# Second-layer weight sums in a lane of their own, GpSimd in program order for two token groups, and closing additions moved into the last products

## The chip, the cores and the metric

One Trainium2 chip, one of its cores. The time is the device time of one execution in microseconds (us), the median of three runs.

The engines by the names of the profile: PE (TensorE matmul, with PEld for its weight loads), DVE (VectorE), ACT (ScalarE), POOL (GpSimd), SP (SyncE, which here issues every DMA).

## The reference, cut to what matters

Three stages follow each other: an attention between tokens and a small state, a two-layer block (`_moe_ref`), and a mixture of eight experts. The change lies in the last one:

```python
def _moe2_ref(x, w_gate, w1, w2):          # x: 2304 x 512 in the signature; 2176 tokens here
    logits = x @ w_gate
    P = np.exp(logits - logits.max())
    for _ in range(8):                      # rows, then columns, eight times
        P /= P.sum(1, keepdims=True) + 1e-09
        P /= P.sum(0, keepdims=True) + 1e-09
        P *= N / E
    for e in range(8):
        h = np.maximum(x @ w1[e], 0.0)      # 512 -> 1024
        out += P[:, e:e + 1] * (h @ w2[e])  # 1024 -> 512
```

All products are made at nearly full float32 precision: a factor is written as a rounded part (hi) and the rest (lo), and three matmuls (hi times lo, hi times hi, lo times hi) stand for one.

## The kernel before, in words

**Units.** The tokens are cut into three groups, g = 0, 1, 2, of 768, 768 and 640 tokens; an expert's 1024 hidden columns are cut into four pieces of 256. One pair of a group and a piece is a unit, s = 0 to 95, with s // 32 the group and s % 32 the piece. `experts()` walks over the units. In this execution unit 0 begins near 444 us, unit 32 near 1030 us, unit 64 near 1498 us.

**PE in a unit.** The first layer of a unit (`quad`) is made with seven block products instead of eight: m1, m6, m5, m7, m2, m4, m3, in this order, six matmuls each, in three banks px, py and pz. m6 leaves its product in py; DVE adds it to m1's (tile u), and only then may m7 accumulate into the same bank py, so m7 waits for that u. In group 0 the second layer is plain: after the first products of a unit stand the six token tiles of the unit before (`layer2_moe`, bank po, six matmuls of 512 columns each). In groups 1 and 2 the second layer has seven products too (`product`, bank pm, order P1, P2, P3, P7, P5, P6, P4), which DVE adds up over the 32 units in the tiles m; after the last unit of a group seven additions between those tiles (`combine`), a transposition (`rows`, bank pt) and the stores give the output.

**Weights in group 0.** `weights_a(s + 1)` and `weights_b(s)` run beside the matmuls of unit s. `weights_a` takes the raw first weights (rw), makes four sums of quarters on POOL (tile sum), and splits weights and sums: hi by ACT (wah, wsh), lo by POOL (wal, wsl). `weights_b` splits the raw second weights (w2h by ACT, w2l by POOL, two pieces of 128x512), makes four sums on DVE (tile sumb, lines L694 to L698) and splits them in two pairs wz_0 and wz_1: hi by ACT (L768), lo by DVE (L769). Everything is also stored to DRAM (`keep`), since groups 1 and 2 load it again (`again`) in place of making it.

**The order.** Between matmul groups `slot()` advances each lane (a list of generators) by one step; a generator's `yield n` says how many slots it rests. A unit of group 0 has 13 slots, one of groups 1 and 2 has 14. `weights_a` and `weights_b` of a unit stand behind each other in lane "w". PE, ACT and, in `experts()`, DVE run in the order in which the code is written; for POOL and SP a scheduler chooses the order when the program is built.

**Memory.** A tile is taken by its tag; tiles of one tag share one place (or `bufs` places in turn), and a new one waits for all readers of the old one, the store by `keep` among them. wz_0 and wz_1 share tag "z" with one place until unit 5; in units 6 to 29 wz_1 lies in "xl5". `sumb` shares "y" with the tile sum until unit 5.

**Late in group 0.** From unit 26 on `sums_of(1)` makes eight differences of 128x384 on DVE for group 1, and in unit 31 `forms(1)` splits the seven token forms of group 1: hi by ACT (L630), lo by DVE (L634, 128x768 each). After group 1 `finish(1)` runs its seven additions on POOL (L976, 128x768) while group 2 computes; after group 2 `finish_last` runs them on DVE and then transposes and stores six row tiles.

Of the kernel before, what the change touches and what calls it, by code (L numbers as in the profile page):

```python
# [19 lines left out]
P = 128  # L20
# [7 lines left out]
FU = 256  # L28
# [16 lines left out]
def body(ctx: ExitStack, tc: tile.TileContext, xt_in, xn_in, stb, stk, wd, ws, alpha, wgate, out):  # L45
# [645 lines left out]
    def sums_left(eng, out, a11, a12, a22, a21):  # L691

        s1, s2, s3, s4 = (out[:, i, :] for i in range(4))
        eng.tensor_tensor(out=s1, in0=a21, in1=a22, op=ALU.add)  # L694
        eng.tensor_tensor(out=s2, in0=s1, in1=a11, op=ALU.subtract)  # L695
        yield 1
        eng.tensor_tensor(out=s3, in0=a11, in1=a21, op=ALU.subtract)  # L697
        eng.tensor_tensor(out=s4, in0=a12, in1=s2, op=ALU.subtract)  # L698
# [31 lines left out]
    def weights_b(s):  # L730
# [23 lines left out]
        if s < 6:  # L754
# [197 lines left out]
    def product(s, i):  # L952
# [26 lines left out]
    def rows(g, h, t0, nt):  # L979

        blocks = [("P2", "P4"), ("P3", "P7")][h]
        ps = p2["tr"].tile([P, 512], F32, tag="tr", name=f"pt{g}_{h}_{t0}")
# [26 lines left out]
    def finish(g):  # L1009

        yield 14
        yield from combine(g, nc.gpsimd, 12)
        yield 12
# [103 lines left out]
    later, soon, lanes = [], [], {"x": [], "state": [], "gate": [], "early": [], "sums": [], "blocks": [], "v": [], "w": [], "h": [], "out": []}  # L1117
# [181 lines left out]
    def experts():  # L1299

        nonlocal pb
        after = ["B11", "T2", "T1", "T3", "B21", "T4", "B22"]
        for s in range(NS2 + 1):
# [20 lines left out]
            if s < NS2:  # L1324
                lanes["w"].append(weights_b(s))
# [102 lines left out]
```

## Time and profile before

| | |
|---|---|
| three runs | 1934.12, 1934.17, 1934.86 us; median 1934.17 us |
| the profiled execution | 1936.51 us, its span 1934.7 us |
| busy, share of the span | PE 94%, PEld 87%, DVE 77%, POOL 64%, ACT 38% |
| granted TensorE clock, mean | 0.971 |

The profile is of one execution. Its span runs from the first to the last instruction; 1.8 us lie around it. Busy shares are means over stages that are limited in different ways, so the rows below are cut by stage, and a stage is read by what PE waits for in it.

### The profile page before, as it was taken

How to read it: one execution, taken by the hardware profiler on the slowest of the kernel's cores; microseconds unless marked ns; L12 is line 12 of the kernel's file. 1: busy time of each engine (PE TensorE's matmuls, PEld its weight loads, DVE VectorE, ACT ScalarE, POOL GpSimd, SP SyncE). 2: the span in 40 equal slices, each digit the busy share in tenths (PEclk: the TensorE clock that was granted, in tenths of full speed). 3: DMA queues.
4: the chain of work that ended last, by engine and by line, in shares of the span. 5: the costliest groups of instructions: out<-in, count | busy, mean ns of one | idle time of the engine just before them, and what ended most of it. 6: DMA issues, size and time to landing. Idle time of an engine off the chain costs nothing.

```text
span 1934.7 us, 29731 instructions
## 1 busy us (share of the span) xinstructions
PE 1813.7 (94%) x10179; PEld 1678.3 (87%) x10179; DVE 1482.3 (77%) x2323; ACT 736.4 (38%) x1397; POOL 1235.8 (64%) x1300
## 2 busy tenths in 40 slices
PE   6799999988889999999999999999999899999997
PEld 5688888876768888888778999999999899999996
DVE  6645777775788888888877777887788777778886
ACT  6755666643223333333332222222223233333332
POOL 4423555565447666666654777777777877777774
PEclk8799999998989999999999999999999899999998
DMA  5111111114557877787778777777777589888882
GB/s 213 44 50 50 50 55 48 41 71 159 206 207 264 289 283 278 281 287 280 256 281 296 248 264 267 247 261 273 250 259 255 199 304 316 315 313 302 304 298 98
DMA packets 179813, 423.82 MB, mean 219 GB/s; under 512 B 20288, under 2 KB 37184, under 8 KB 179664
## 3 DMA queue, kind: packets, MB, share of 16 engines
q1 hardware_dynamic: 179664, 421.94, 61.7%
q8 instruction: 81, 1.33, 0.3%
q14 instruction: 68, 0.56, 0.1%
HBM read 299.92 MB, written 121.94 MB: 218 GB/s over the span
## 4 chain that ended last, share of the span: by engine, by line
PE 48%; POOL 12%; issue 7%; DVE 5%; DMA 3%; ACT 1%; SPq 0%; POOLq 0%; ACTq 0%; DVEq 0%
PE pm L964 22%; PE py L801 10%; PE px L801 7%; PE pz L801 7%; POOL wsl L671 3%; POOL w2l L671 3%; PE po L1071 3%; POOL wal L671 2%; DMA kept_bl<-wz 2%; POOL sum L694 1%; POOL sum L695 1%; POOL sum L697 1%; DVE g2l L824 1%; DMA rw<-in_ws_dram 1%; PE pt L984 0%
## 5 line engine op out<-in xcount | busy, mean ns | idle before, releaser
L970 DVE TENSOR_TENSOR m<-pm,m 128x768 f32<-128x768 f32 (+1 forms) x434 | 384.0, 885 | 136.4 <-PE pm L964 136.0
L964 PE MATMUL pm<-formgh,wz 128*128 128x384 f32 (+1 forms) x1152 | 216.5, 323 | 0.7 <-POOL formgh L905 0.5
L801 PE MATMUL py<-rT,wsh 128*128 128x384 f32 (+1 forms) x768 | 193.8, 335 | 24.8 <-DVE u L808 24.8
L895 POOL TENSOR_TENSOR formgh<-mid,formgh 128x384 fp32r<-128x384 f32 (+1 forms) x128 | 121.7, 952 | 123.4 <-ACT formgh L894 102.4
L964 PEld LDWEIGHTS pm<-formgh,wz 128*128 128x128 f32 x1152 | 190.1, 188 | 1.3 <-POOL formgh L905 0.7
L801 PE MATMUL px<-rB,wah 128*128 128x384 f32 (+1 forms) x768 | 190.3, 330 | 0.2 <-DVE c L808 0.2
L823 ACT ACTIVATE g2h<-c 128x384 fp32r<-128x384 f32 x96 | 50.4, 525 | 335.2 <-DVE c L808 335.2
L801 PEld LDWEIGHTS py<-rT,wsh 128*128 128x128 f32 x768 | 136.2, 191 | 37.0 <-DVE u L808 36.1
L536 POOL TENSOR_TENSOR gl<-r,gh 128x512 fp32r<-128x512 f32 (+1 forms) x80 | 94.2, 1191 | 115.0 <-ACT gh L535 61.8
L671 POOL TENSOR_TENSOR wal<-rw,wah 128x256 fp32r<-128x256 f32 x96 | 77.1, 830 | 128.9 <-ACT wah L669 94.0
L1071 PE MATMUL po<-w2h,g2l 128*128 128x512 f32 x384 | 153.2, 399 | 2.0 <-DVE g2l L824 1.8
L1071 PE MATMUL po<-w2l,g2h 128*128 128x512 f32 x384 | 154.9, 403 | 0.0
L1071 PE MATMUL po<-w2h,g2h 128*128 128x512 f32 x384 | 154.2, 402 | 0.0
L801 PEld LDWEIGHTS px<-rB,wah 128*128 128x128 f32 x768 | 138.1, 191 | 6.8 <-DVE c L808 0.5
L905 POOL TENSOR_TENSOR T<-mid,mid 128x384 f32<-128x384 f32 (+1 forms) x128 | 119.8, 958 | 30.4 <-DVE mid L889 30.4
L894 ACT ACTIVATE formgh<-mid 128x384 fp32r<-128x384 f32 (+1 forms) x128 | 63.9, 499 | 181.6 <-DVE mid L889 131.6
L551 PE MATMUL po<-gl,wh 128*128 128x512 f32 (+1 forms) x320 | 120.4, 377 | 13.1 <-DVE acc L568 11.1
L1093 DVE SCALAR_TENSOR_TENSOR oa<-po,pr,oa 128x512 f32<-128x512 f32 x168 | 122.8, 742 | 10.2 <-PE po L1071 9.6
L801 PE MATMUL py<-rT,wsl 128*128 128x384 f32 (+1 forms) x384 | 126.9, 330 | 0.0
L801 PE MATMUL px<-rB,wal 128*128 128x384 f32 (+1 forms) x384 | 126.2, 329 | 0.0
L964 PE MATMUL pm<-formgl,w2h 128*128 128x384 f32 (+1 forms) x512 | 123.3, 324 | 2.3 <-DVE m L970 2.3
L905 POOL TENSOR_TENSOR T<-mid,T 128x384 f32<-128x384 f32 (+1 forms) x128 | 121.7, 951 | 5.1
(240 smaller groups left out, 5126.5 us busy)
## 6 DMA issues: line engine op xcount, KB each, us to landing
wsh<-kept_ah SPq DMA_DIRECT2D x64, 512.0 KB, 4.5
wsl<-kept_al SPq DMA_DIRECT2D x64, 512.0 KB, 5.4
wz<-kept_bh SPq DMA_DIRECT2D x128, 256.0 KB, 5.0
wz<-kept_bl SPq DMA_DIRECT2D x128, 256.0 KB, 5.1
wah<-kept_ah SPq DMA_DIRECT2D x64, 384.0 KB, 3.2
wal<-kept_al SPq DMA_DIRECT2D x64, 384.0 KB, 3.8
w2h<-kept_bh SPq DMA_DIRECT2D x64, 384.0 KB, 6.0
w2l<-kept_bl SPq DMA_DIRECT2D x64, 384.0 KB, 6.6
```

Of the source, the lines that this page charges most:

```text
L536: nc.gpsimd.tensor_tensor(out=lo, in0=r, in1=f32(hi), op=ALU.subtract)
L551: nc.tensor.matmul(ps, lhsT=w2(wt, u, f, d * P, P), rhs=g[:, f, :n], start=(i == 0), stop=(i == 3 * NF - 1))
L671: nc.gpsimd.tensor_tensor(out=lo[:, i], in0=src[:, i], in1=f32(hi[:, i]), op=ALU.subtract)
L801: nc.tensor.matmul(bank[b], lhsT=w[:, k * P:(k + 1) * P], rhs=xf[:, j, k, :], start=(first and i == 0), stop=(i == 5), skip_group_check=True,)
L823: nc.scalar.activation(out=hi, in_=src, func=AF.Relu)
L894: nc.scalar.activation(out=hi, in_=out, func=AF.Copy)
L895: nc.gpsimd.tensor_tensor(out=lo, in0=out, in1=f32(hi), op=ALU.subtract)
L905: nc.gpsimd.tensor_tensor(out=out, in0=x, in1=y, op=ALU.subtract)
L964: nc.tensor.matmul(ps[:, q, :n], lhsT=w[:, q * P:(q + 1) * P], rhs=x, start=(j == 0), stop=(j == 2))
L970: nc.vector.tensor_tensor(out=mm[g][name], in0=ps[:, :, :n], in1=mm[g][name], op=ALU.add)
L1071: nc.tensor.matmul(ps, lhsT=x[:, f, t * P:(t + 1) * P], rhs=w[:, f, :], start=(i == 0), stop=(i == 3 * NF - 1))
L1093: nc.vector.scalar_tensor_tensor(out=a, in0=ps, scalar=p, in1=a, op0=ALU.mult, op1=ALU.add)
```

## The change

1. `weights_b` gets a lane of its own, "w2", from unit 2 on, so that it begins at the first slot of a unit, beside `weights_a`. Its four sums are spread over four slots, and the hi of a pair (ACT) and its lo (DVE) stand one slot apart.
2. wz_1 lies in "xl3" (units 2 to 25) or "xl5" (26 to 30), apart from wz_0; `sumb` lies in "xh5" from unit 2 on. For that the broadcast row tile pb is taken at unit 31 in place of 30, and its loads are issued one unit ahead in place of two.
3. The lo parts of the forms T2, T3 and T4 of group 1 move from DVE to POOL.
4. From unit 32 on POOL runs in the order of the code.
5. `finish(1)` rests 20 slots and then 14 between additions (before: 14 and 12).
6. The seven closing additions of group 2 are moved: two to POOL and three to DVE within the last unit's products, two to DVE between the two halves of the rows. The rows of the last group take turns in the two places of bank m, and the second tile of each half is copied out by DVE.

```diff
@@ forms(g): put
-                nc.vector.tensor_tensor(out=t[:, 1, part], in0=src[:, part], in1=f32(t[:, 0, part]), op=ALU.subtract)
+                eng = nc.gpsimd if g == 1 and name in ("T2", "T3", "T4") else nc.vector
+                eng.tensor_tensor(out=t[:, 1, part], in0=src[:, part], in1=f32(t[:, 0, part]), op=ALU.subtract)
@@ weights_b
-        if s < 6:
+        if s < 2:
             sums = p2["t"].tile([P, 4, FU], F32, tag="y", name=f"sumb{s}", bufs=1)
...
-        yield from sums_left(nc.vector, sums, halves[:, 0, 0], halves[:, 1, 0], halves[:, 1, 1], halves[:, 0, 1])
+        yield from sums_left(nc.vector, sums, halves[:, 0, 0], halves[:, 1, 0], halves[:, 1, 1], halves[:, 0, 1], 1)
...
-            if i and 6 <= s < U2 - 2:
-                z = big.tile([P, 2, 2, FU], F32R, tag="xl5", name=f"wz_{s}_{i}")
+            if i and s >= 2 and s != U2 - 1:
+                z = big.tile([P, 2, 2, FU], F32R, tag="xl3" if s < U2 - 6 else "xl5", name=f"wz_{s}_{i}")
...
             nc.scalar.activation(out=hi, in_=src, func=AF.Copy)
+            yield 1
             nc.vector.tensor_tensor(out=lo, in0=src, in1=f32(hi), op=ALU.subtract)
             keep(u, "b", (hi, lo), 3 + 2 * i)
-            yield 2
+            yield 1
@@ product
+        if s == NS2 - 1:
+            for eng, after, x, y in (
+                (nc.gpsimd, "P2", "P2", "P1"), (nc.gpsimd, "P5", "P3", "P5"), (nc.vector, "P6", "P6", "P1"),
+                (nc.vector, "P6", "P7", "P6"), (nc.vector, "P6", "P4", "P7"),
+            ):
+                if after == name:
+                    join(eng, g, x, y)
@@ finish
-        yield 14
-        yield from combine(g, nc.gpsimd, 12)
-        yield 12
+        yield 20
+        yield from combine(g, nc.gpsimd, 14)
@@ finish_last
-        for _ in combine(g, nc.vector, 0):
-            pass
...
+            if h:
+                join(nc.vector, g, "P7", "P5")
+                join(nc.vector, g, "P3", "P6")
...
+                if k == 1:
+                    nc.vector.tensor_copy(out=t[:nt], in_=ps[:nt])
+                else:
+                    nc.scalar.activation(out=t[:nt], in_=ps[:nt], func=AF.Copy)
@@ experts
+            if s == U2:
+                pool_order = tc.manual_schedule(engines={mybir.EngineType.Pool})
+                pool_order.__enter__()
...
-                lanes["w"].append(weights_b(s))
+                lanes["w2" if s > 1 else "w"].append(weights_b(s))
```

What it does to the order is shown at three places. In the rows g2l is the lo of the hidden layer, c and u are sums of products, oa the output rows, and the number behind a name is the unit.

DVE in the second half of unit 12, up to the u that m6 of unit 13 needs, before:

```order
L698 TENSOR_TENSOR sumb_6347<-rw_12_6198,sumb_6347 128x256
L808 TENSOR_TENSOR c_12_6367<-py_6255,p_12_6246 128x384
L769 TENSOR_TENSOR wz_0_6372<-sumb_6347,wz_0_6372 128x512
L1093 SCALAR_TENSOR_TENSOR oa_4301<-po_11_4_6377,pr,oa_4301 128x512
L824 SCALAR_TENSOR_TENSOR g2l_6238<-c_12_6367,g2h_6237 128x384
L808 TENSOR_TENSOR c_12_6392<-pz_6282,u_12_6262 128x384
L769 TENSOR_TENSOR wz_1_6395<-sumb_6347,wz_1_6395 128x512
L1093 SCALAR_TENSOR_TENSOR oa_4301<-po_11_5_6400,pr,oa_4301 128x512
L824 SCALAR_TENSOR_TENSOR g2l_6238<-c_12_6392,g2h_6237 128x384
L808 TENSOR_TENSOR u_13_6434<-py_6427,p_13_6418 128x384
```

and after:

```order
L775 TENSOR_TENSOR wz_0_6347<-sumb_6293,wz_0_6347 128x512
L1116 SCALAR_TENSOR_TENSOR oa_4301<-po_11_3_6359,pr,oa_4301 128x512
L830 SCALAR_TENSOR_TENSOR g2l_6238<-px_6239,g2h_6237 128x384
L814 TENSOR_TENSOR c_12_6376<-py_6266,p_12_6246 128x384
L775 TENSOR_TENSOR wz_1_6368<-sumb_6293,wz_1_6368 128x512
L1116 SCALAR_TENSOR_TENSOR oa_4301<-po_11_4_6382,pr,oa_4301 128x512
L830 SCALAR_TENSOR_TENSOR g2l_6238<-c_12_6376,g2h_6237 128x384
L814 TENSOR_TENSOR c_12_6397<-pz_6295,u_12_6273 128x384
L1116 SCALAR_TENSOR_TENSOR oa_4301<-po_11_5_6400,pr,oa_4301 128x512
L830 SCALAR_TENSOR_TENSOR g2l_6238<-c_12_6397,g2h_6237 128x384
L814 TENSOR_TENSOR u_13_6445<-py_6438,p_13_6418 128x384
```

Both lo steps moved up by three to four instructions, and their hi is now issued on ACT one slot earlier; the sums, which stood in the middle of the unit, now begin behind its first oa.

POOL around the start of unit 12 (sum and wal, wsl of unit 13's first weights, w2l of the second weights), before:

```order
L694 TENSOR_TENSOR sum_6252<-rw_13_6133 128x256
L697 TENSOR_TENSOR sum_6252<-rw_13_6133 128x256
L695 TENSOR_TENSOR sum_6252<-sum_6252,rw_13_6133 128x256
L698 TENSOR_TENSOR sum_6252<-rw_13_6133,sum_6252 128x256
L671 TENSOR_TENSOR w2l_6149<-rw_11_6026,w2h_6148 128x512 x2
L671 TENSOR_TENSOR wal_6249<-rw_13_6133,wah_6248 128x256 x3
L671 TENSOR_TENSOR wsl_6251<-sum_6252,wsh_6250 128x256 x4
```

and after:

```order
L695 TENSOR_TENSOR sum_6252<-rw_13_6147 128x256
L700 TENSOR_TENSOR sum_6252<-rw_13_6147 128x256
L698 TENSOR_TENSOR sum_6252<-sum_6252,rw_13_6147 128x256
L703 TENSOR_TENSOR sum_6252<-rw_13_6147,sum_6252 128x256
L672 TENSOR_TENSOR w2l_6256<-rw_12_6173,w2h_6255 128x512 x2
L672 TENSOR_TENSOR wal_6249<-rw_13_6147,wah_6248 128x256 x3
L672 TENSOR_TENSOR wsl_6251<-sum_6252,wsh_6250 128x256 x4
```

The same seven rows, but the w2l in front of wal is now that of the running unit, half a unit earlier than before.

POOL in the last unit (T are differences of token blocks, formgl and formgh the lo parts that the products wait for, m the summed products), before:

```order
L905 TENSOR_TENSOR T_95_19793<-mid_0_19720,mid_1_19756 128x320
L905 TENSOR_TENSOR T_95_19795<-mid_1_19756,mid_0_19720 128x320
L905 TENSOR_TENSOR T_95_19807<-mid_0_19720,T_95_19795 128x320
L905 TENSOR_TENSOR formgl_9820<-T_95_19793,formgl_9820 128x320
L905 TENSOR_TENSOR formgh_9884<-T_95_19795,formgh_9884 128x320
L905 TENSOR_TENSOR T_95_19819<-mid_1_19756,T_95_19807 128x320
L905 TENSOR_TENSOR formgh_9884<-T_95_19807,formgh_9884 128x320
L905 TENSOR_TENSOR formgl_9885<-T_95_19819,formgl_9885 128x320
```

and after:

```order
L911 TENSOR_TENSOR T_95_19795<-mid_0_19722,mid_1_19758 128x320
L911 TENSOR_TENSOR T_95_19797<-mid_1_19758,mid_0_19722 128x320
L1039 TENSOR_TENSOR m_2_14925<-m_2_14925 128x640
L911 TENSOR_TENSOR formgl_9822<-T_95_19795,formgl_9822 128x320
L911 TENSOR_TENSOR T_95_19810<-mid_0_19722,T_95_19797 128x320
L911 TENSOR_TENSOR formgh_9886<-T_95_19797,formgh_9886 128x320
L911 TENSOR_TENSOR T_95_19822<-mid_1_19758,T_95_19810 128x320
L911 TENSOR_TENSOR formgh_9886<-T_95_19810,formgh_9886 128x320
L1039 TENSOR_TENSOR m_2_14925<-m_2_14925,m_2_14926 128x640
L911 TENSOR_TENSOR formgl_9887<-T_95_19822,formgl_9887 128x320
```

Two additions of 128x640 now stand in front of lo parts that the products P7 and P4 wait for.

## Rows read from the trace of the kernel before

**Rows 1.** The page's head: the span.

```profile
span 1934.7 us, 29731 instructions
```

**Rows 2.** Windows: length, busy PE, PEld, DVE, ACT, POOL (count), clock, DMA, GB/s.

```profile
490.70:582.40 91.70, 75.37 (x344) 64.95 (x343) 74.21 (x161) 26.27 (x47) 43.61 (x52) 0.91 0.56 206
582.40:917.70 335.30, 319.39 (x1571) 280.04 (x1570) 281.44 (x421) 123.39 (x226) 233.85 (x264) 1.00 0.79 281
917.70:1043.50 125.80, 114.23 (x534) 99.04 (x533) 103.72 (x159) 42.41 (x76) 62.76 (x68) 0.96 0.77 273
1512.60:1548.80 36.20, 29.63 (x170) 29.04 (x171) 23.94 (x34) 7.36 (x16) 31.29 (x30) 0.86 0.57 202
1548.80:1561.10 12.30, 12.30 (x86) 12.30 (x85) 9.85 (x17) 3.75 (x8) 9.39 (x12) 1.00 0.82 297
1896.40:1934.70 38.30, 24.94 (x144) 21.03 (x143) 21.15 (x31) 9.20 (x18) 15.73 (x19) 0.79 0.18 56
```

**Rows 3.** Waits, 582.4 to 917.7: who for whom, us, times, longest.

```profile
DVE wz L769 <- ACT wz L768: 45.2, 40, 1.5
...
PE py L801 <- DVE u L808: 15.8, 19, 1.5
```

**Rows 4.** Chain of waits: start, us, what; one group of six matmuls each.

```profile
639.11 1.04 PE px L801 x6
640.15 1.39 PE po L1071 x6
```

**Rows 5.** Windows of the instructions on sumb alone: length, busy DVE, ACT.

```profile
582.40:917.70 335.30, 104.85 (x120) 24.62 (x41) 1.00 0.79 281
```

**Rows 6.** The tile sumb: duration in ns, shortest, median, longest.

```profile
L769 DVE TENSOR_TENSOR wz<-sumb,wz x64: 679/693/1750, 461.5 to 1022.8; 128x512 fp32r<-128x512 f32 x64
...
L698 DVE TENSOR_TENSOR sumb<-rw,sumb x32: 410/1507/1514, 460.0 to 1017.0; 128x256 f32<-128x256 f32 x32
```

**Rows 7.** POOL's groups by line, 582.4 to 917.7: busy, mean ns, idle before.

```profile
L671 POOL TENSOR_TENSOR w2l<-rw,w2h 128x512 fp32r<-128x512 f32 x40 | 58.4, 1481 | 0.0
L671 POOL TENSOR_TENSOR wsl<-sum,wsh 128x256 fp32r<-128x256 f32 x80 | 57.2, 749 | 0.0
L671 POOL TENSOR_TENSOR wal<-rw,wah 128x256 fp32r<-128x256 f32 x60 | 48.2, 830 | 93.7 <-ACT wah L669 58.9 <-DMA kept_bl<-wz 34.8
```

**Rows 8.** DMA issues, 582.4 to 917.7: KB each, median us to landing.

```profile
rw<-in_ws_dram SPq DMA_DIRECT2D x20, 512.0 KB, 4.5
```

**Rows 9.** The tile w2h, 582.4 to 917.7, its writer on ACT.

```profile
L669 ACT ACTIVATE w2h<-rw x20: 1044/1047/1049, 589.6 to 906.9; 128x1024 fp32r<-128x1024 f32 x20
```

**Rows 10.** Waits, 917.7 to 1043.5.

```profile
DVE wz L769 <- ACT wz L768: 15.2, 11, 4.5
...
PE py L801 <- DVE u L808: 11.3, 7, 2.8
```

**Rows 11.** Line L634 (lo of the forms), 1010 to 1032.

```profile
L634 DVE TENSOR_TENSOR rT<-sxl,rT x3: 946/958/1393, 1014.6 to 1027.3; 128x768 fp32r<-128x768 f32 x3
```

**Rows 12.** Waits, 490.7 to 582.4.

```profile
PE pcs L459 <- DVE cs L456: 14.2, 4, 5.9
...
DVE wz L769 <- ACT wz L768: 8.4, 6, 2.3
```

**Rows 13.** PE's waits, 1512.6 to 1548.8.

```profile
PE pm L964 <- POOL formgl L905: 3.8, 1, 3.8
PE pm L964 <- POOL formgh L895: 2.8, 1, 2.8
```

**Rows 14.** POOL's groups by line, 1480 to 1549.

```profile
L976 POOL TENSOR_TENSOR m<-m,m 128x768 f32<-128x768 f32 x4 | 7.3, 1836 | 0.0
```

**Rows 15.** POOL in order of time, last unit.

```profile
1910.90 0.86 POOL L905 TENSOR_TENSOR formgl<-T,formgl 128x320 fp32r<-128x320 f32 x1
```

**Rows 16.** Chain of waits at the end.

```profile
1916.38 0.82 DVE m L970
...
1920.44 0.70 PE pt L984 x2
1921.14 0.02 issue
1921.16 0.61 ACT stage L1033
1921.77 0.04 issue
1921.82 1.13 PE pt L984 x4
```

More of the change, by code (lines that the diff above doesn't have):

```diff
@@ L689, in name_left, with sums_left @@
             into[name, s] = [base[j][:, i, :] if i < 3 else pairs[(i - 3) // 2][j][:, (i - 3) % 2, :] for j in range(2)]
-    def sums_left(eng, out, a11, a12, a22, a21):
+    def sums_left(eng, out, a11, a12, a22, a21, gap=0):
         s1, s2, s3, s4 = (out[:, i, :] for i in range(4))
         eng.tensor_tensor(out=s1, in0=a21, in1=a22, op=ALU.add)
+        if gap:
+            yield gap
         eng.tensor_tensor(out=s2, in0=s1, in1=a11, op=ALU.subtract)
@@ L697, in sums_left @@
         eng.tensor_tensor(out=s3, in0=a11, in1=a21, op=ALU.subtract)
+        if gap:
+            yield gap
         eng.tensor_tensor(out=s4, in0=a12, in1=s2, op=ALU.subtract)
@@ L981, in rows @@
         blocks = [("P2", "P4"), ("P3", "P7")][h]
-        ps = p2["tr"].tile([P, 512], F32, tag="tr", name=f"pt{g}_{h}_{t0}")
+        if g == NG - 1:
+            ps = p2["m"].tile([P, 2, 512], F32, tag="m", name=f"pt{g}_{h}_{t0}")[:, 0]
+        else:
+            ps = p2["tr"].tile([P, 512], F32, tag="tr", name=f"pt{g}_{h}_{t0}")
         for i in range(KD):
@@ L1021, in finish, with join @@
                 yield 5
+    def join(eng, g, x, y):
+        eng.tensor_tensor(out=mm[g][x], in0=mm[g][x], in1=mm[g][y], op=ALU.add)
     def finish_last(g):
-        for _ in combine(g, nc.vector, 0):
-            pass
         stage = big.tile([P, 6, DM], F32, tag="acc0", name="stage")
@@ L1029, in finish_last @@
         for h in range(2):
-            for t0, nt in cuts(g, h):
+            parts = list(cuts(g, h))
+            if h:
+                join(nc.vector, g, "P7", "P5")
+                join(nc.vector, g, "P3", "P6")
+            for k, (t0, nt) in enumerate(parts):
                 ps = rows(g, h, t0, nt)
                 t = stage[:, i, :]
-                nc.scalar.activation(out=t[:nt], in_=ps[:nt], func=AF.Copy)
+                if k == 1:
+                    nc.vector.tensor_copy(out=t[:nt], in_=ps[:nt])
+                else:
+                    nc.scalar.activation(out=t[:nt], in_=ps[:nt], func=AF.Copy)
                 store(g, h, t0, nt, t)
@@ L1116, in body @@
     made = {}
-    later, soon, lanes = [], [], {"x": [], "state": [], "gate": [], "early": [], "sums": [], "blocks": [], "v": [], "w": [], "h": [], "out": []}
+    later, soon, lanes = [], [], {"x": [], "state": [], "gate": [], "early": [], "sums": [], "blocks": [], "v": [], "w": [], "w2": [], "h": [], "out": []}
     wait = dict.fromkeys(lanes, 0)
@@ L1299, in experts @@
     def experts():
-        nonlocal pb
+        nonlocal pb, pool_order
         after = ["B11", "T2", "T1", "T3", "B21", "T4", "B22"]
@@ L1313, in experts @@
                 flush("early")
-            if s == U2 - 2:
+            if s == U2 - 1:
                 pb = big.tile([P, 2, 768], F32, tag="xl5", name="pb")
-            if s % UE == UE - 2 and U2 - 2 <= s < NS2 - 2:
-                load_p((s + 2) // U2, (s + 2) % U2 // UE)
+            if s % UE == UE - 1 and U2 - 1 <= s < NS2 - 1:
+                load_p((s + 1) // U2, (s + 1) % U2 // UE)
+            if s == U2:
+                pool_order = tc.manual_schedule(engines={mybir.EngineType.Pool})
+                pool_order.__enter__()
             if s == U2 + 1:
@@ L1351, in experts @@
                     slot()
-            for lane in ("w", "sums", "blocks"):
+            for lane in ("w", "w2", "sums", "blocks"):
                 flush(lane)
@@ L1355, in experts @@
         finish_last(NG - 1)
-    pb = None
+        pool_order.__exit__(None, None, None)
+    pb = pool_order = None
     start()
```

## The prediction, made before the changed kernel was run

> **What bounds the kernel now.** I read the windows by stage first, then what PE waits for in each, then DVE, POOL and the DMA rows of the stages where PE waits. The sum is made against the profiled execution: 1936.5 us, span 1934.7 [rows 1], with 1.8 us around it; the median of the runs is 2.3 us lower, and I take 2.3 off at the end. In units 7 to 25, and in all of groups 1 and 2 but their edges, PE does nearly everything: the window 582.4 to 917.7 (20 units, 16.77 us each) has PE busy 319.4 of 335.3 us [rows 2], and the window of unit 67 has it busy for 12.30 of 12.30 [rows 2]. A steady unit of groups 1 and 2 can therefore gain nothing. What there is to win lies in five places.
>
> A unit of group 0 is seven groups of px, py, pz at 1.04 and six of po at 1.39 [rows 4], so 7.28 + 8.34 = 15.62 us when PE never stops. That is the **floor**. The 20 units stand 22.9 us above 20 floors; 15.8 of it is PE waiting for DVE's u, once in nearly every unit [rows 3], and the rest lies in weight loads behind that wait. DVE is busy only 281.4 us, 14.07 a unit [rows 2], yet it is late. It waits 45.2 us, 2.26 a unit in two pieces, for the hi of wz, which ACT makes only when DVE has finished the sums [rows 3]. So 14.07 + 2.26 = 16.33 of 16.77 us of DVE are taken, and PE's wait is the return leg of this loop.
>
> **The change part by part.**
>
> *Sums spread, hi and lo a slot apart (units 2 to 30).* The order shows the lo of wz three to four DVE instructions further from its sums, and a hi takes ACT 24.62 / 41 = 0.60 us [rows 5], less than a slot (1.04 or 1.39). The 2.26 us of waiting should vanish. But the sums move to the start of the unit, where POOL is working on sum, w2l and wal; before, they ran in its middle. What neighbours cost them is visible now: the six instructions on sumb take 104.85 us in 20 units, 5.24 a unit [rows 5], while the same forms have been seen from 0.41 to 1.51 (L698) and from 0.68 to 1.75 us (L769) [rows 6]. If every sum took the shortest, a unit would need 4 x 0.41 + 2 x 0.68 = 3.0; if every one took the longest, 4 x 1.51 + 2 x 1.75 = 9.5. I put them between the middle, 6.25, and the point given by POOL's busy share, 233.85 / 335.3 = 0.70 [rows 2], 3.0 + 0.70 x 6.5 = 7.55. DVE then has 14.07 + 1.0 to 14.07 + 2.3, that is 15.1 to 16.4 us of work against PE's 15.62. At the lower end PE never stops, at the upper DVE sets 16.4; I take 16.0, the middle of 15.62 and 16.4.
> The Trainium skill, page "SBUF — State Buffer", section "Who interferes with whom", says that GpSimd reads and writes SBUF through a pair of ports that is DVE's second pair, and that whichever instruction holds it excludes the other. By that rule, DVE's two-input sums and POOL's subtractions should be kept apart in time, and this change puts them together. The trace agrees that one form of one size takes either 0.41 or 1.5 us [rows 6], but no row here says who held what.
>
> - Units 6 to 25: 20 x (16.77 - 16.0) = **-15.4** us. Bounds: -23 (floor) and 0.
> - Units 2 to 5 (490.7 to 582.4): the wz waits are 8.4 us here [rows 12] and go; four units give back 1.0 to 2.3 each of it in longer sums where DVE is the late one. PE's larger wait there, 14.2 for the state's DVE step [rows 12], is not touched by the edits, though shorter queues on DVE may help it. **-4**; bounds -8.4 and 0.
> - Units 26 to 32 (917.7 to 1043.5, 125.8 us): the waits are the same two, wz 15.2 and py 11.3 [rows 10]. The three lo forms on DVE, 0.95 to 1.39 us [rows 11], go to POOL, which has room (62.8 of 125.8 busy [rows 2]): -3.3 on DVE. DVE's work becomes 103.7 - 3.3 + 7 x (1.0 to 2.3) = 107 to 116.5, PE's floor is 7 x 15.62 = 109.3. Take 114.5 = **-11**; bounds -16.5 and -4. If POOL is late with the lo forms (three of 128x768 at the 1.84 of [rows 14] are 5.5 us), the first products of group 1 wait; that is inside the upper bound.
>
> *Places and loads.* wz_1 and sumb get places of their own, which only removes waits. pb's loads are issued one unit (12 us or more) ahead in place of two; the slowest median in these rows is 4.5 us from issue to landing [rows 8]. Nothing, with the whole unit as cover; without it some 4 us at unit 32 once.
>
> *The weights' loop.* weights_b of unit s now begins at its start, so w2l stands in front of wal on POOL. The loop is: raw second weights land (4.5 us [rows 8]), hi on ACT 1.05 [rows 9], then on POOL two w2l, three wal and four wsl, 2.96 + 2.49 + 3.0 = 8.45 [rows 7], then the store and SP's queue, in which the next load stands behind it. 4.5 + 1.05 + 8.45 + some 0.5 = 14.5, inside a unit of 15.62 to 16, so I cost it at nothing. The margin is only 1.1 us; it is the first rival.
>
> *Group 1's closing additions.* Units 65 and 66 take 36.2 us against 2 x 12.30 for two steady ones [rows 2], 11.6 too much, at a clock of 0.86 [rows 2]. PE waits 3.8 and 2.8 us in them for lo parts on POOL [rows 13], in front of which stand four additions m<-m,m of 1.84 us each, back to back [rows 14]. The scheduler had collected them there. In code order with a gap of 14 slots, there is one in a unit: POOL 9.39 [rows 2] + 1.84 = 11.2 of 12.3 us. PE's waits vanish, and with them the low clock that stands in the same window. **-10.5**; bounds -12 and -6. Code order may place something else badly in groups 1 and 2, where I see no wait now; POOL has 2.9 us a unit to absorb it.
>
> *The end.* Before, DVE makes its additions after the last product (0.82 each [rows 16]) and then transposes alternate with ACT's copies: 0.70 pt, 0.61 copy, 1.13 pt, and so on [rows 16]. With two banks in turn and two copying engines, five gaps of 0.65 (0.61 plus issue) shrink by some 3.3 us. Against it: two additions of 128x640 on POOL stand ahead of lo parts (0.86 us for 128x320 [rows 15], 1.84 for 128x768 [rows 14], so some 1.6 each), and each first waits for DVE's last sum into m. P7 and P4 come 1.7 to 2 us later, and the second half of the rows waits for two DVE additions, 0.9 us more of it uncovered. -3.3 + 1.9 + 0.9 is about -0.5, with the clock at 0.79 [rows 2]: **0**; bounds -2 and +2.
>
> Sum: -15.4 - 4 - 11 - 10.5 + 0 = -41, so 1936.5 - 41 = 1895.5 profiled, and 1893 as a median (the 2.3 us off). The bounds together give -62 and -10, which are not reached all at once; the forecast's own range is 1874 to 1905.
>
> **The rivals.**
>
> R1, *the weights' loop binds.* If the load takes 6 instead of 4.5 us, or POOL's instructions stretch beside DVE's sums, the loop's 14.5 becomes 16.3 or so. For: margin 1.1 us, wal idles 34.8 us already for a store [rows 7], and the DMA share is 0.79 [rows 2]. Against: before, the same work fits in 16.77 with POOL idle 30%. At 16.3 a unit: units 6 to 25 20 x (16.77 - 16.3) = -9.4, units 26 to 32 -6, 2 to 5 -2, group 1's edge -10.5: -28, so 1906 as a median. Chance 0.20.
>
> R2, *slower: DVE's sums and POOL's subtractions collide.* If all six on sumb go to their longest, DVE has 14.07 - 5.24 + 9.5 = 18.3 us a unit. Then 20 x 1.6 = +32, units 26 to 32 +8, 2 to 5 +3, group 1's edge -10.5: +32, so 1966. It makes the kernel slower only from about 3.2 us more a unit on (17.3; 26 units x 0.5 then eat the 10.5 won at group 1's edge). For: L698 is at 1.51 in the median already [rows 6], and the sums move to where POOL works. Against: POOL is idle 30% of the time, so not all six can meet it. The skill's rule of the shared ports, named above, leads here if it holds for every pair of instructions. Chance 0.08, 1938 to 1966.
>
> R3, *the change doesn't do what it says.* The lo of wz still waits, on the store of the tile that had the place before or on an ACT that is itself behind, and group 0 keeps 16.77. Then only group 1's edge is left: 1934.2 - 10.5 = 1924. Against: ACT is busy 123 of 335 us [rows 2]. Chance 0.06.
>
> R4, *given back.* Group 0 gains a little, and POOL in code order or the end loses as much: within 0.2% of 1934 (3.9 us, about what a measurement of this kernel can tell). Chance 0.04.
>
> **How the numbers follow.** Forecast 0.62 (1893, 1874 to 1905), R1 0.20 (1906), R3 0.06 (1924), R4 0.04, R2 0.08. The range goes from the forecast's low end to R3's time: 1874 to 1924 leaves out R2, R4 and a little at either end, just under 0.2. Faster 0.62 + 0.20 + 0.06 = 0.88, same 0.04, slower 0.08.
>
> **What the profile after would show.** The wait of DVE's wz for ACT's hi gone; PE's wait for u down to under 0.4 us a unit; 20 units like 6 to 25 in about 320 us. Under R1 POOL has no idle time but that for DMA, and PE's first wait is for wal, wsl or their products' weights. Under R2 the six on sumb sum to over 8 us a unit and PE waits for u longer than 0.8 us. No PE wait for a POOL form in units 65 and 66, clock 1.00 there. At the end PE waits longer for formgl and its transposes follow each other at about 1.1 us. I am wrong if units of group 0 stay above 16.4 us, if group 1's edge keeps its waits, or if a steady unit of group 2 grows past 12.30.

## The result and the profile after

The changed kernel takes 1887.4 us in the median (1886.36 to 1891.43), the kernel before 1934.1: a ratio of 0.976 with an interval of 0.9745 to 0.9779. 1893 was forecast, in a range of 1874 to 1924. The page's head of the changed kernel, and the windows of the stages that answer to [rows 2]; columns as there.

```profile
span 1885.8 us, 29666 instructions
...
492.20:575.80 83.60, 71.74 (x322) 61.69 (x321) 75.99 (x162) 25.10 (x47) 49.35 (x56) 0.92 0.64 228
575.80:887.70 311.90, 311.90 (x1562) 279.92 (x1561) 288.69 (x422) 125.72 (x226) 246.29 (x260) 1.00 0.84 301
887.70:1005.60 117.90, 112.32 (x547) 99.19 (x546) 105.69 (x154) 42.19 (x75) 70.76 (x71) 0.99 0.82 292
1474.90:1499.50 24.60, 24.60 (x170) 24.60 (x169) 20.09 (x32) 7.49 (x16) 20.54 (x23) 1.00 0.83 296
1847.70:1885.80 38.10, 25.38 (x144) 22.12 (x142) 21.62 (x31) 7.98 (x16) 18.62 (x21) 0.80 0.18 56
```

The five windows are units 2 to 5, 6 to 25, 26 to 32, 65 and 66, and the end. In the second, PE is busy for 311.90 of 311.90 us: the floor. From PE's first matmul of a unit to that of the next it is 15.64 us in 18 of the 20 units. The edges of the windows, here and in [rows 2], are the starts of ACT's `p<-px`, of which a unit has one. ACT comes to it 1 to 10 us after PE's first matmul of the unit, and not equally late before and after. Unit 6 before, then unit 2 after:

```profile
577.20 0.51 PE L801 MATMUL px<-rB,wah 128*128 128x384 f32 x2
582.36 0.47 ACT L830 ACTIVATE p<-px 128x384 f32<-128x384 f32 x1
...
487.37 0.62 PE L807 MATMUL px<-rB,wah 128*128 128x384 f32 x2
492.19 0.47 ACT L836 ACTIVATE p<-px 128x384 f32<-128x384 f32 x1
```

So the stages of before and after are compared with these edges, as everywhere below, and in the last column with PE's first matmuls as edges:

| stage | before, us | after, us | difference | forecast | difference by PE's edges |
|---|---|---|---|---|---|
| up to unit 2 | 490.7 | 492.2 | +1.5 | 0 | -1.7 |
| units 2 to 5 | 91.7 | 83.6 | -8.1 | -4 | -3.1 |
| units 6 to 25 | 335.3 | 311.9 | -23.4 | -15.4 | -22.5 |
| units 26 to 32 | 125.8 | 117.9 | -7.9 | -11 | -10.6 |
| units 33 to 62 | 436.9 | 436.9 | 0 | 0 | 0 |
| units 63 to 66 | 68.4 | 57.0 | -11.4 | -10.5 | -11.4 |
| units 67 to 94 | 347.6 | 348.1 | +0.5 | 0 | +0.5 |
| the end | 38.3 | 38.1 | -0.2 | 0 | -0.2 |

The start of the first row is not the change's: unit 0 began between 441 and 446 us in all the profiles of this study, with the same code ahead of it. Nor are two stages fixed by their code alone. Units 26 to 32, with the same code there, took 125.8 us in the kernel before and 122.9 to 123.5 in the three experiments below that leave group 0 alone; the changed kernel took 117.9 and, profiled again, 115.5. Units 63 to 66 with their waits took 65.6 to 68.4 us in five profiles. A single profile is therefore good to some 3 us in these two. The experiments are compared stage by stage, and kernels that ran together by their ratio to the kernel before among them.

The waits in units 6 to 25 after, sorted by sum (who for whom, us, times, longest):

```profile
...
POOL w2l L672 <- ACT w2h L670: 57.7, 17, 7.9
DVE oa L1116 <- PE po L1094: 14.9, 21, 0.9
...
DVE u L814 <- PE py L807: 6.4, 10, 0.9
```

Neither row of [rows 3] is left. DVE no longer waits for ACT's hi, and PE for nothing; DVE now waits for PE, 14.9 and 6.4 us. So the bound has passed from DVE to PE. POOL idles 57.7 us for ACT's w2h, nearly 3 us a unit: the weights' loop has room.

Yet the six instructions on sumb became dearer, as the prediction feared (duration in ns, shortest, median, longest; to be read against [rows 6] and the sum of [rows 5]):

```profile
L775 DVE TENSOR_TENSOR wz<-sumb,wz x40: 1026/1190/1230, 583.9 to 884.2; 128x512 fp32r<-128x512 f32 x40
...
L698 DVE TENSOR_TENSOR sumb<-sumb,rw x20: 425/1400/1552, 578.9 to 876.4; 128x256 f32<-128x256 f32 x20
L700 DVE TENSOR_TENSOR sumb<-rw x20: 406/997/1133, 580.9 to 877.8; 128x256 f32<-128x256 f32 x20
L703 DVE TENSOR_TENSOR sumb<-rw,sumb x20: 597/606/611, 582.3 to 879.8; 128x256 f32<-128x256 f32 x20
```

The lo of wz rose from 0.69 to 1.19 us in the median, but the last sum (L698 before, L703 after) fell from 1.51 to 0.61. The groups of DVE by line give 117.6 us for the six, 5.88 a unit against 5.24: +0.64. All of DVE is 288.69 / 20 = 14.43 a unit, 1.2 under PE's 15.6.

### The profile page after: what moved, and what is told of

The parts are those of the page before. It is cut to its first block, busy times and chain, and to the rows that moved or that the text cites. A ratio compares the mean times of both kernels' runs of the same rounds, so it can differ in the third digit from the quotient of the medians.

```text
span 1885.8 us, 29666 instructions
## 1 busy us (share of the span) xinstructions
PE 1799.4 (95%) x10179; PEld 1674.5 (89%) x10179; DVE 1497.8 (79%) x2320; ACT 735.9 (39%) x1395; POOL 1264.0 (67%) x1305
## 3 DMA queue, kind: packets, MB, share of 16 engines
q8 instruction: 81, 1.33, 0.3%
## 4 chain that ended last, share of the span: by engine, by line
PE 67%; DVE 6%; DMA 1%; issue 0%; ACT 0%; POOL 0%; SPq 0%; ACTq 0%; DVEq 0%
PE pm L970 22%; PE py L807 14%; PE po L1094 12%; PE px L807 9%; PE pz L807 9%; DMA kept_bl<-wz 1%; DVE g2l L830 1%; DVE wz L775 1%; DVE oa L1112 0%; DVE m L976 0%; PE pt L1000 0%; DVE c L814 0%; DVE rT L635 0%; DVE u L814 0%; DVE sumb L698 0%
## 5 line engine op out<-in xcount | busy, mean ns | idle before, releaser
L807 PE MATMUL py<-rT,wsh 128*128 128x384 f32 (+1 forms) x768 | 189.5, 329 | 1.0 <-DVE u L814 0.9
L672 POOL TENSOR_TENSOR w2l<-rw,w2h 128x512 fp32r<-128x512 f32 x64 | 86.9, 1380 | 116.7 <-ACT w2h L670 102.1
L895 DVE SCALAR_TENSOR_TENSOR mid<-mid,pb 128x384 f32<-128x384 f32 (+1 forms) x192 | 120.7, 629 | 6.6
L807 PE MATMUL py<-rT,wsl 128*128 128x384 f32 (+1 forms) x384 | 125.8, 328 | 0.0
```

Source lines behind the costliest of these rows:

```text
L672: nc.gpsimd.tensor_tensor(out=lo[:, i], in0=src[:, i], in1=f32(hi[:, i]), op=ALU.subtract)
L807: nc.tensor.matmul(bank[b], lhsT=w[:, k * P:(k + 1) * P], rhs=xf[:, j, k, :], start=(first and i == 0), stop=(i == 5), skip_group_check=True,)
L895: nc.vector.scalar_tensor_tensor(out=out, in0=src, scalar=0.0, in1=pb[:, e % 2, h * n:(h + 1) * n], op0=ALU.max, op1=ALU.mult)
```

## The experiments

Three questions were open. Which edit removed the wait? What does the crowding of DVE and POOL cost, and from where on? And why did units 26 to 32 and the end give less than they could?

**Only the lane, slots and places.** The edit is items 1 and 2 of the change:

```diff
-                lanes["w"].append(weights_b(s))
+                lanes["w2" if s > 1 else "w"].append(weights_b(s))
...
+            yield 1
             nc.vector.tensor_tensor(out=lo, in0=src, in1=f32(hi), op=ALU.subtract)
```

> The kernel before with only the lane, the slots, the places and the pb loads of the change (items 1 and 2). Theory: this is what gained the 23.4, 8.0 and most of the 7.9 us in units 6 to 25, 2 to 5 and 26 to 32; the time is 1934 - 23.4 - 8 - 7 = about 1896 (1893 to 1899), and units 65 and 66 keep their waits for POOL's lo parts. Rival: GpSimd's order or the lo forms on POOL did part of it in group 0; then units 6 to 25 stay above 15.9 us each and the time is above 1902.

Measured: 1893.0, a ratio of 0.9804 (0.9774 to 0.9835). By stage: units 2 to 5 -8.4, 6 to 25 -23.2, 26 to 32 -7.8, and units 65 and 66 keep their waits of 3.8 and 2.8 us. These items made all of the gain up to unit 25. Whether the lo forms on POOL (item 3) added to units 26 to 32 is not settled: 118.0 us here without them, 117.9 and 115.5 in the two profiles of the changed kernel.

**Only GpSimd's order and the rests.** Items 4 and 5:

```diff
+            if s == U2:
+                pool_order = tc.manual_schedule(engines={mybir.EngineType.Pool})
+                pool_order.__enter__()
...
-        yield 14
-        yield from combine(g, nc.gpsimd, 12)
-        yield 12
+        yield 20
+        yield from combine(g, nc.gpsimd, 14)
```

> The kernel before with only POOL in code order from unit 32 and the longer rests between closing additions (items 4 and 5). Theory: units 65 and 66 fall from 36.2 to about 24.7 us and nothing else moves: -11.4, about 1923 (1921 to 1925). Rival: the waits there came with group 0's late end, so that alone this brings under 6 us: above 1928.

Measured: 1923.4, 0.9965 (0.9947 to 0.9983). Units 63 to 66 went from 68.4 to 57.1 us, the +0.5 of units 67 to 94 came with it, and the units from 2 to 25 did not move. The kernel before that ran beside it took 1929.7 us, so the gain is 6.3 us, with an interval of 3.3 to 10.2, where 11.4 was expected; that 1923 came out as expected is owed to the lower base. Against the other profiles with the waits, units 63 to 66 gained 8.5 to 10.1 us.

**Only the rests**, with the second of those two pieces alone:

> The kernel before with only the longer rests between the closing additions of group 1 (item 5), POOL still in the scheduler's order. Theory: the scheduler collects the additions as before, the waits of 3.8 and 2.8 us in units 65 and 66 stay, and the time is within 2 us of the kernel before; so the code order is what gained the 11.4. Rival: the rests alone spread them; then 8 to 12 us faster.

Measured: 1.0014 (1.0001 to 1.0027), so no gain. The seven additions still stand within 23 us (1504.4 to 1527.3), singly or two behind each other, and PE waits for the lo parts behind them (two of the additions, then PE's waits):

```profile
1523.35 1.84 POOL L976 TENSOR_TENSOR m<-m,m 128x768 f32<-128x768 f32 x1
1525.16 2.10 POOL L976 TENSOR_TENSOR m<-m 128x768 f32<-128x768 f32 x1
...
PE pm L964 <- POOL formgl L905: 3.8, 1, 3.8
...
PE pm L964 <- POOL formgh L895: 1.7, 1, 1.7
```

So the code order is needed; the rests alone win nothing, because the scheduler collects the additions whatever slot they were written in. In code order, with the rests, one stands in a unit. Whether the order does it without the longer rests was not run.

**Only hi and lo a slot apart**, in the old lane and at the old place of the unit:

```diff
             nc.scalar.activation(out=hi, in_=src, func=AF.Copy)
+            yield 1
             nc.vector.tensor_tensor(out=lo, in0=src, in1=f32(hi), op=ALU.subtract)
             keep(u, "b", (hi, lo), 3 + 2 * i)
-            yield 2
+            yield 1
```

> The kernel before with one edit: the hi of a wz pair and its lo stand one slot apart, in the old lane and at the old place of the unit. Theory A: the wait for ACT inside DVE's order was the whole cause, wherever it stands; then DVE's wait for the hi falls from 45 to under 5 us, units 6 to 25 come to 15.6 to 15.8 us each, and the time falls by 18 to 25 us to 1909 to 1916. Theory B: the early start of the lane is what frees DVE; then the wait vanishes but most of PE's wait for u stays, and the gain is under 8 us.

Measured: 1898.9, 0.9831 (0.9801 to 0.9861). Units 2 to 5 -7.6, units 6 to 25 -21.1, units 26 to 32 -7.0: by the stages one moved line gives about nine tenths of what the first experiment gave, by the medians 31 of 37 us. The 2 us that are missing in units 6 to 25 stand in unit 6 alone, whose PE idles 1.9 us. The reason is read from DVE and ACT in order of time. First the kernel before, around the first lo of a unit:

```profile
645.18 0.55 DVE L808 TENSOR_TENSOR c<-py,p 128x384 f32<-128x384 f32 x1
646.84 0.69 DVE L769 TENSOR_TENSOR wz<-sumb,wz 128x512 fp32r<-128x512 f32 x1 [1.11 <-ACT wz L768]
...
645.75 0.53 ACT L823 ACTIVATE g2h<-c 128x384 fp32r<-128x384 f32 x1 [4.97 <-DVE c L808]
646.19 0.62 ACT L768 ACTIVATE wz<-sumb 128x512 fp32r<-128x512 f32 x1
```

The hi (646.19) does not wait for the sums, whose last ended at 645.26 (its row is shown further below). It stands on ACT behind g2h, and g2h waits for the c that DVE has just made. So DVE makes c, and then waits for g2h and hi, 1.11 us, twice a unit. The same place with the slot between:

```profile
646.09 0.55 DVE L809 TENSOR_TENSOR c<-py,p 128x384 f32<-128x384 f32 x1
646.56 0.73 DVE L1094 SCALAR_TENSOR_TENSOR oa<-po,pr,oa 128x512 f32<-128x512 f32 x1
647.23 0.56 DVE L825 SCALAR_TENSOR_TENSOR g2l<-c,g2h 128x384 fp32r<-128x384 f32 x1
647.75 0.69 DVE L770 TENSOR_TENSOR wz<-sumb,wz 128x512 fp32r<-128x512 f32 x1
...
646.67 0.53 ACT L824 ACTIVATE g2h<-c 128x384 fp32r<-128x384 f32 x1 [5.88 <-DVE c L809]
647.10 0.62 ACT L768 ACTIVATE wz<-sumb 128x512 fp32r<-128x512 f32 x1
```

Two instructions of DVE, oa and g2l, now run while ACT does g2h and hi.

**The slot taken back**, the lane kept: the two lines above, in the other direction, in the changed kernel.

> The changed kernel with one edit taken back: hi and lo of a wz pair again in one slot (the lane, the places and the early start stay). Theory A (the wait for ACT inside DVE's order is the cause, wherever it stands): DVE waits again some 1.1 us per pair, has 14.4 + 2.2 = 16.6 us taken in a unit, and units 6 to 25 go back to 16.3 to 16.8 us: +14 to +23 us, 1901 to 1911. Theory B (early in the unit DVE has slack that hides the wait): units 6 to 25 stay under 15.9 and the time within 5 us of the changed kernel.

Measured: 1885.0, 0.9763 (0.9738 to 0.9788), and units 6 to 25 at 311.9 us, the same as with the slot. Theory A in its strict form falls: not the slot is needed, but work between. With the early lane, hi and lo come into a slot where oa and g2l stand between c and lo anyway, and DVE shows no wait for the hi:

```profile
672.38 0.56 DVE L813 TENSOR_TENSOR c<-pz,u 128x384 f32<-128x384 f32 x1
...
673.39 0.74 DVE L1115 SCALAR_TENSOR_TENSOR oa<-po,pr,oa 128x512 f32<-128x512 f32 x1
674.05 0.54 DVE L829 SCALAR_TENSOR_TENSOR g2l<-c,g2h 128x384 fp32r<-128x384 f32 x1
674.51 1.23 DVE L774 TENSOR_TENSOR wz<-sumb,wz 128x512 fp32r<-128x512 f32 x1
```

So the slot alone nearly suffices, the early lane (with its places and spread sums, which were not taken apart) suffices without the slot, and together they win no more.

**POOL emptied.** In the changed kernel, for the weights numbered 6 to 25:

```diff
         for i in range(src.shape[1]):
+            if on_act:
+                nc.scalar.activation(out=lo[:, i], in_=src[:, i], func=AF.Copy)
+                continue
             nc.gpsimd.tensor_tensor(out=lo[:, i], in0=src[:, i], in1=f32(hi[:, i]), op=ALU.subtract)
```

> The changed kernel with POOL's lo parts wal, wsl and w2l of the weights with numbers 6 to 25 replaced by plain copies on ACT of the same shapes (the remainder of the rounding is left out, so the output is not the reference's). POOL then has only the four sums in a unit, about 3.6 us of 15.6. Theory (DVE's two-input instructions are long where POOL works at the same time): L775 falls from 1.19 to about 0.69 us in the median, and the six on sumb from 5.9 to about 3.0 to 4 us a unit; units stay at 15.6, since PE is at its floor. Rival (their length comes from the operands or from DVE's own queue): L775 stays near 1.19 and the six above 5.5.

Measured in one run, units 6 to 25:

```profile
L778 DVE TENSOR_TENSOR wz<-sumb,wz x40: 673/1188/1227, 580.3 to 881.4; 128x512 fp32r<-128x512 f32 x40
...
L703 DVE TENSOR_TENSOR sumb<-rw x20: 414/415/436, 576.6 to 875.0; 128x256 f32<-128x256 f32 x20
L706 DVE TENSOR_TENSOR sumb<-rw,sumb x20: 573/576/859, 578.1 to 876.5; 128x256 f32<-128x256 f32 x20
```

Three of the sums (two others like L703) are at 0.42 us, about the shortest seen. The six come to 38.5 + 37.4 = 75.9 us in the groups by line, 3.8 a unit, as expected; but half of the lo of wz stayed at 1.2, against the letter of the theory. I laid each instruction over POOL's in units 7 to 24, in this kernel, the changed one and the one before: no long instruction on sumb (over 0.47 us for 128x256, over 0.72 for 128x512) was without a POOL instruction beside it. Here the 18 lo of 0.67 us have none beside them, and the 18 of 1.22 us have one of POOL's four remaining sums. The reverse does not hold: in the changed kernel 8 of 72 sums took 0.41 to 0.46 us although POOL was subtracting beside them; in each of the eight the subtraction that outlasted the sum began at most 0.02 us before it, or later. The theory holds instruction by instruction, and the rival falls; the expectation missed where POOL's sums would stand. How a long one looks, in the kernel before (POOL, then DVE):

```profile
643.50 2.92 POOL L671 TENSOR_TENSOR w2l<-rw,w2h 128x512 fp32r<-128x512 f32 x2
...
643.75 1.51 DVE L698 TENSOR_TENSOR sumb<-rw,sumb 128x256 f32<-128x256 f32 x1
```

The DVE sum begins a quarter of a microsecond after the first of two POOL subtractions of some 1.46 us and ends 0.28 us after that one does. This is so without exception in units 7 to 24: all 73 long instructions on sumb before and all 97 in the changed kernel end 0.28 to 0.29 us (128x256) or 0.55 us (128x512) after the end of a POOL instruction that had begun before them. POOL's wsl, 0.75 us in the mean [rows 7], takes 0.93 in the changed kernel: 0.97 where an instruction on sumb runs beside it, 0.74 where none does. So the delay is mutual. The units stay at 15.64 us by PE's edges, as PE is at its floor either way.

**The lo of wz made twice**, in the changed kernel:

```diff
-            nc.vector.tensor_tensor(out=lo, in0=src, in1=f32(hi), op=ALU.subtract)
+            for _ in range(2 if 6 <= s < 26 else 1):
+                nc.vector.tensor_tensor(out=lo, in0=src, in1=f32(hi), op=ALU.subtract)
```

> The changed kernel with the lo of wz made twice over, one after the other, in units 6 to 25: 2 x 1.16 = 2.3 us more DVE work a unit. Theory (DVE has 15.6 - 14.43 = 1.2 us to spare and becomes the bound past that): units 6 to 25 at 16.6 to 16.9 us, +20 to +26, about 1907 to 1914. Rival (PE waits only through the one u, and the doubled work stands where DVE is ahead): under 16.1 us a unit, less than +10.

Measured: 1911.1, 0.9903 (0.9888 to 0.9918). The window of units 6 to 25, and the longer of PE's two waits in it:

```profile
572.70:914.40 341.70, 324.92 (x1573) 279.24 (x1572) 338.88 (x461) 123.19 (x226) 243.86 (x260) 1.00 0.79 276
...
PE px L808 <- DVE g2l L831: 10.4, 17, 0.9
```

DVE is busy for 338.9 of 341.7 us, and a unit takes 17.09: DVE's 16.94 and a little. Against the changed kernel, 2.5 us more work on DVE cost 1.5 us a unit. So DVE had about 1 us to spare, and past that it sets the time. It came out 0.2 above the expected 16.9: the sums met POOL more often too, 71 of 72 long in units 7 to 24 where 61 were, L695 in the mean at 1.33 us in place of 0.89.

**Only the end.** Item 6 in the kernel before, POOL in the scheduler's order:

```diff
+                (nc.gpsimd, "P2", "P2", "P1"), (nc.gpsimd, "P5", "P3", "P5"), (nc.vector, "P6", "P6", "P1"),
+                (nc.vector, "P6", "P7", "P6"), (nc.vector, "P6", "P4", "P7"),
...
-        for _ in combine(g, nc.vector, 0):
-            pass
```

> The kernel before with only the end changed (item 6). Theory: what the two banks and the early additions win (some 5 us after the last product) is lost by the two additions on POOL that hold up the last products (4.8 us): within 2 us of 1934. Rival: the end loses nothing and the -0.2 us seen there is the low clock; then this alone is 3 us or more faster.

Measured: 0.999 (0.9971 to 1.0009); the end takes 36.3 us in place of 38.3. That is at the edge of what was expected, and the trace shows why it is not nothing. The scheduler set the two additions behind the last lo part:

```profile
1906.02 0.88 POOL L905 TENSOR_TENSOR formgl<-T,formgl 128x320 fp32r<-128x320 f32 x1
1906.86 1.57 POOL L1034 TENSOR_TENSOR m<-m 128x640 f32<-128x640 f32 x1
1908.38 2.11 POOL L1034 TENSOR_TENSOR m<-m,m 128x640 f32<-128x640 f32 x1
```

In the changed kernel, where item 4 has POOL follow the code, the first stands in front of a lo part (POOL, then PE):

```profile
1862.36 1.53 POOL L1039 TENSOR_TENSOR m<-m 128x640 f32<-128x640 f32 x1 [1.15 <-DVE m L976]
1863.85 0.86 POOL L911 TENSOR_TENSOR formgl<-T,formgl 128x320 fp32r<-128x320 f32 x1
...
1864.76 1.14 PE L970 MATMUL pm<-formgl,wz 128*128 128x320 f32 x6 [2.46 <-POOL formgl L911]
```

POOL idles 1.15 us for DVE, adds for 1.53, and only then makes the lo part for which PE waits 2.46 us. With the second addition, PE waits 5.2 us for POOL's lo parts at the end, against 1.2 before. Items 4 and 6 are each a gain, and together they take 1.9 us of it back.

**Both remaining waits removed.** In unit 31 the chain of waits of the changed kernel runs:

```profile
978.70 1.95 DVE wz L775
980.66 4.92 DMA kept_bl<-wz
...
985.69 0.64 ACT wz L773
...
986.35 0.69 DVE wz L775
...
987.71 2.06 DVE g2l L830
...
989.81 1.48 PE po L1094 x3
```

This is R3's mechanism in one unit: wz_1 of unit 31 is the only one from unit 2 on without a place of its own, and its hi waits until wz_0 has been stored, 4.92 us. Before, the like stood in unit 30, where DVE's longest wait of [rows 10], 4.5 us, is for a hi that waits for a store; the change gave that unit's wz_1 a place. The edit:

```diff
+            elif i and s == U2 - 1:
+                z = p2["t"].tile([P, 2, 2, FU], F32R, tag="y", name=f"wz_{s}_{i}", bufs=1)
...
-                (nc.gpsimd, "P2", "P2", "P1"), (nc.gpsimd, "P5", "P3", "P5"), (nc.vector, "P6", "P6", "P1"),
+                (nc.vector, "P2", "P2", "P1"), (nc.gpsimd, "P4", "P3", "P5"), (nc.vector, "P6", "P6", "P1"),
```

> The changed kernel with two edits: wz_1 of unit 31 lies in the place of POOL's sum (tag y), which nothing uses then, and of the closing additions P2+P1 goes to DVE and P3+P5 to POOL behind the last lo part. Theory: the 4.6 us for which PE waits in unit 31 come from wz_1 waiting for the store of wz_0 out of the same place, and the 4 to 5 us for POOL's lo parts at the end come from the additions in front of them; so units 26 to 32 fall from 117.9 to about 112 us and the end from 38.1 to about 34.5: 8 to 10 us below the changed kernel, 0.995 of it. Rival: PE only waits for the next late thing (DVE's forms in unit 31, DVE's additions at the end), and less than 4 us is won.

> The changed kernel unaltered, as the yardstick for the three beside it: 0.976 of the kernel before (0.9745 to 0.9779).

Measured side by side: the changed kernel 1883.4 (0.9757, 0.9736 to 0.9778), this one 1877.7 (0.9731, 0.9709 to 0.9753). It is 5.7 us lower in the median; the intervals overlap, so the gain is not clear by the times alone. The traces say where: PE's wait of 4.6 us in unit 31 (2.7 in the second profile of the changed kernel) is gone, units 26 to 32 take 112.9 us against 117.9 and 115.5, and the end 35.3 against 38.1 in both. Less than the 8 to 10 expected. PE's waits at the end now:

```profile
PE pt L1002 <- DVE m L978: 3.2, 1, 3.2
PE pm L972 <- POOL formgh L913: 1.3, 2, 0.9
PE pt L1002 <- DVE m L1041: 1.3, 1, 1.3
```

POOL's 5.2 us are down to 1.3, and the transposes' waits for DVE's additions grew from 2.3 to 4.5. So at the end part of the rival was right: the products are finished early and DVE is next.

**Both additions on POOL, but late:**

```diff
-                (nc.gpsimd, "P2", "P2", "P1"), (nc.gpsimd, "P5", "P3", "P5"), (nc.vector, "P6", "P6", "P1"),
+                (nc.gpsimd, "P6", "P2", "P1"), (nc.gpsimd, "P6", "P3", "P5"), (nc.vector, "P6", "P6", "P1"),
```

> As e11_both, but both additions that the change put on POOL stay there and only stand behind the last lo part. Theory: the products come as early as with P2+P1 on DVE, and what follows waits for the two on POOL; the end is 36 to 36.5 us (as with the scheduler's order, 36.3), 1.5 to 2 us more than in e11_both. Rival: it is the work on POOL as such, not its place, that costs; then the end stays at 38.

Measured in one run: the end takes 36.7 us, PE's wait for POOL's lo parts is 0.7, and the transposes wait 5.5 for DVE. That is 0.2 above what was expected, and by its theory: the place of the additions costs, not the work on POOL. Units 26 to 32, with the new place, took 110.7 us here.

**Item 3 taken back:**

```diff
-                eng = nc.gpsimd if g == 1 and name in ("T2", "T3", "T4") else nc.vector
-                eng.tensor_tensor(out=t[:, 1, part], in0=src[:, part], in1=f32(t[:, 0, part]), op=ALU.subtract)
+                nc.vector.tensor_tensor(out=t[:, 1, part], in0=src[:, part], in1=f32(t[:, 0, part]), op=ALU.subtract)
```

> The changed kernel with item 3 taken back (the lo parts of T2, T3 and T4 of group 1 on DVE again). Theory: in unit 31 DVE waits for the place of wz_1 anyway, so 3 us more work on it costs 0 to 1.5 us in units 26 to 32 (117.9). Rival: DVE is the bound there; then 3 us or more.

Measured in one run: units 26 to 32 take 118.0 us, and PE's wait for g2l in unit 31 is 3.9. In the changed kernel's two profiles it is 117.9 us with a wait of 4.6, and 115.5 with 2.7. So three microseconds less work on DVE bought 0 to 2.5 us there; the theory that they are lost in DVE's wait for a store agrees with the first profile and is not shown by the second.

## Why the prediction was right, step by step

- **What bounds the kernel.** Right. The loop of DVE and ACT behind [rows 3] was the bound; it is gone, and PE is the bound, at the floor worked out from [rows 4]: 15.62 forecast, 15.64 measured. The account of the loop was loose in one point: the hi was late not because of the sums but because of g2h in front of it on ACT, which waits for DVE's c.
- **Units 6 to 25.** The mechanism was right and the size off: -23.4 (-22.5 by PE's edges) against -15.4, at the stated bound. The term that was mis-sized is the cost of crowding: +0.64 us a unit on the six sumb instructions measured, +1.0 to +2.3 put in. The median of one instruction was taken to move up with the others; in the new order one of the six fell by 0.9 us, which made up for most of the rise of the lo by 0.5 each. And DVE at 14.43 stays 1.2 under PE, so its cost came to nothing.
- **Units 2 to 5.** The size was right by luck. Of the -8.1 against -4, 5.0 are moved edges; PE gained 3.1. It did not gain them where the prediction sought them: PE waited for u 0.6 us there before and 0.7 after, so the wz waits of [rows 12] had cost PE next to nothing directly. What shrank is the wait for the state's step, from 14.2 [rows 12] to 10.9 us, for which the prediction had only a "may help".
- **Units 26 to 32.** -7.9, or -10.6 by PE's edges, against -11, in a stage that varies by some 3 us: near the forecast. The 3.3 us credited to the lo forms on POOL brought 0 to 2.5, and a wait for a store was overlooked, which the longest of [rows 10], 4.5 us, had shown in unit 30 and which the new places leave in unit 31.
- **Units 65 and 66.** The four units from 63 on gave -11.4 against -10.5, by the mechanism named; it needed the code order. [rows 14] was misread: the additions did not stand back to back but singly and in pairs, seven within 23 us, and the two or three in front of each late lo part were enough.
- **The end.** -0.2 against 0, but two errors met. The products end 25.2 us after the unit's start in place of 19.9: +5.3, where 1.7 to 2 had been priced; POOL's wait for DVE's sum was named there but not priced. What follows the products then took 13 us in place of 18.4, where -3.3 + 0.9 had been priced.
- **The rivals.** R1 did not come: POOL waits nearly 3 us a unit for ACT's w2h, and the load takes 4.7 us. R2's mechanism is real, as the emptied POOL shows, but it added 0.64 us and not 4.3; with the lo doubled the price beyond the slack is as R2 put it, one for one. R3 held in unit 31 alone. R4: items 4 and 6 took 1.9 us from each other.
- **The sum.** The median came in at 1887.4, 6 us below the forecast. Units 6 to 25, with the crowding put in too high, are 7.1 us of that by PE's edges, and the other stages give about one back. The upper bounds of the five places add up to -8, not -10; the range does not rest on it.

## What to carry to other kernels

When an in-order engine makes X, waits for another engine's Y and that Y is queued behind something that needs X, two independent instructions between X and the user of Y remove the wait; one slot of distance alone gave 31 us, where the change with six parts gave 45 to 47. Before crediting relief to an engine, look at whether it waits at that very place for something else: in unit 31 it waited for a store. And when work is moved to an engine in program order, look at what stands behind it there at the moment when it must wait for its own input.

## What the runs showed of the hardware

A DVE instruction with two operands in SBUF took 0.42 us (128x256) with no POOL instruction beside it, and up to 1.55 us beside a POOL subtraction. Every long one ended 0.28 us after one of POOL's that had begun earlier (0.55 us for 128x512), so it waited for that one instruction and not for POOL's queue. POOL's own wsl went from 0.75 to 0.93 us. The Trainium skill, page "SBUF — State Buffer", section "Who interferes with whom", says that DVE's second pair of ports is GpSimd's and is held exclusively. The traces agree: the long ones all have a POOL instruction beside them that began first, and in the eight short ones the POOL instruction that outlasted them began with them or after.

The same wait of PE can cost different amounts. Unit 66 with its wait of 2.78 us was profiled in three kernels in which its code is the same (the kernel before, hi and lo a slot apart, and the end alone; columns as in [rows 2]):

```profile
1530.70:1548.80 18.10, 15.35 (x86) 15.35 (x87) 11.52 (x19) 3.74 (x8) 13.27 (x16) 0.81 0.57 204
...
1490.80:1507.70 16.90, 14.13 (x86) 14.13 (x87) 11.55 (x19) 3.74 (x8) 13.37 (x16) 0.90 0.59 216
...
1525.30:1540.60 15.30, 12.57 (x86) 12.57 (x87) 11.48 (x19) 3.73 (x8) 13.62 (x16) 1.00 0.67 240
```

With the granted clock at 0.81, 0.90 and 1.00 of full speed on average, the same 86 matmuls took 15.35, 14.13 and 12.57 us. So up to 2.8 of the 11.4 us that units 63 to 66 gave back are the clock after a wait, and vary from one execution to the next.
